# Two-level Strassen mixture of experts on one Trainium2 core: another order of the postponed sums on VectorE, the shares loaded in halves, one more empty place in a list

## The chip, the cores and the metric

The kernel runs on one core of one Trainium2 chip. The metric is the time of one execution on the device in microseconds; of the kernel before there are three runs, and their median counts. One more execution was recorded by the profiler. The engines are named as the profile names them: PE (TensorE, the matrix multiplier), PEld (the loads of its weights, which run beside it), DVE (VectorE), ACT (ScalarE), POOL (GpSimd) and SP (SyncE, which issues most transfers). Each engine works through its own instructions in the order in which they were issued, and waits on semaphores for the others.

## What is computed

Three stages in a row, in float32 throughout:

```python
x = attention(q, k_pooled, v_pooled)            # 4 batches x 576 tokens = 2304 tokens, 512 wide
P = exp(x @ w_gate - max)                       # 2304 x 8 experts
for _ in range(8):                              # Sinkhorn: rows, then columns
    P /= P.sum(1); P /= P.sum(0); P *= 2304 / 8
y = sum(P[:, e] * (relu(x @ w1[e]) @ w2[e]) for e in range(8))     # w1: 512 x 1024, w2: 1024 x 512
out = softplus(y @ w_in) @ w_out                # 512 x 2048, 2048 x 512
```

Nearly all of the time goes into the matrix products of the last two lines. Each float32 product is made of three products of rounded parts: high by high, high by low, low by high, where "low" is the remainder that is left when the high part is taken away.

## The kernel before

**Phases and units.** The 2304 tokens are three parts of 768. The six phases are the experts on part 0, on part 1 and on part 2, and then the softplus layer on parts 1, 2 and 0. In an expert phase there are 32 units, four for each expert, and a unit is 256 columns of the hidden layer. `first` makes a unit's hidden activations, `second` multiplies them by the second matrix and adds into the result.

**Strassen.** A unit's first product is cut into 2 x 2 blocks, and seven block products take the place of eight, at the price of sums of blocks on the other engines. In the phases of parts 1 and 2 (`TWICE`) this is done for the second product too, over two units together, an even one and the odd one behind it: seven products that are called forms 0 to 6 here.

**One pair, in PE's order.** `first_twice` of the even unit makes A11, A22, S2, S1, A12 and S3 (lines 852 to 875). Then `second_twice` of the odd unit of the pair before makes that pair's form 2; `go_on` brings the even unit's seventh product, S4; forms 3 to 6 follow. Then the odd unit comes in the same way, with forms 0 and 1 of its own pair around its S4. Each of the block products is six matrix multiplications of 384 columns, each form twelve.

**The sums of a unit on DVE.** The products lie in PSUM in two tiles of two banks each, d1 (pa and pd) and d2 (pc and pb). ACT copies A11 to `a`. DVE then makes `u1 = pb + a` (row `u<-p,za` in the profile), after S2 and S1, and PE may add S3 onto pb only when u1 has been read. After S3 DVE makes `a = pb + a` (`za<-p,za`), `pb = pc + a` and `pd = pd + a` (both `p<-p,za`, pb's first). PE may add S4 onto pc only when `pb = pc + a` has read pc. After S4 comes `pc = pc + u1` (`p<-p,u`).

**Forms out of sums.** `even_posts` and `odd_posts` multiply the positive part of d1 and d2 by the tokens' shares (`shared`, `p<-p,pb` or `a<-p,pb`; `pb` is here the tile that holds one expert's 768 shares on every partition) and build the seven left factors. The last four steps of the odd unit are put off: the list `later` (line 954) holds s2 (form 5: a cast on ACT, a remainder on POOL), s4 (form 6: `d1 = d1 - s3` on DVE, row `p<-p,s`, then a cast on ACT), s1 (form 4: `a21 = d2 + a21` on DVE, row `a<-p,a`, then a cast on ACT, a remainder on POOL), and form 6's remainder on DVE (`hlo<-p,hhi`, which needs the cast of s4). `first_twice` of the next even unit issues them: the first two ahead of u1, the other two right behind it (lines 860 to 869).

**Shares.** `load_shares` brings the next expert's 768 shares in one transfer by SP, at the end of each fourth unit, when `p2` of that unit has read the old ones. `p1` of the next even unit reads the first half of them, `p2` the second.

**Side work.** While the first phase runs, `hook` takes one entry at a time from the list `side` at fixed places between the products; an entry of None is an empty place. The Sinkhorn steps stand in it: `sk_max` (a maximum on DVE), an empty place, `sk_max_t` (a transpose on PE, row `pm<-ident,big`), and so on. When the list is empty the same places serve the conversion of the last weights from float64 (`convert`).

Of the kernel before, what the change touches and what calls it, by code (L numbers as in the profile page):

```python
# [19 lines left out]
def attention_moe_softplus_kernel(  # L20
# [12 lines left out]
    nc = tc.nc  # L33
    B, H, S, D = q.shape
    N, DM = out.shape
    E = w_gate.shape[1]
# [7 lines left out]
    P = 128  # L44
# [12 lines left out]
    UPE = FF // US  # L57
# [4 lines left out]
    LARGE = max(PAIRS)  # L62
# [110 lines left out]
    TWICE = (1, 2)  # L173
    FORMS = 7
    TB = LARGE // 2
# [6 lines left out]
    pb = []  # L182
    sd = {u: dram.tile([P, 4, 2, P], F32, name=f"sd{u}") for u in range(NU1)}
    td = {d: dram.tile([P, 4, UC, HALF], F32, name=f"td{d}") for d in range(NU1 // 2)}
    pd = dram.tile([sum(PAIRS[1:]) // P * E, P], F32, name="pd")
# [8 lines left out]
    def pair_of_units(n):  # L194
        return TWICE.index(sets[n][0]) * NU1 // 2 + sets[n][3] // 2
# [48 lines left out]
        pool_sub(lo, raw_form(q), hi.bitcast(F32))  # L244
        load_form(q + 4)

    def load_shares(i):
        if i < len(TWICE) * E:
            m, e = divmod(i, E)
            n = LARGE // P  # L250
            src = pd.rearrange("(t e) p -> e t p", e=E)[e, m * n:(m + 1) * n]
            nc.sync.dma_start(
                pb[0].rearrange("p (t n) -> p t n", n=P), src.partition_broadcast(P)
            )

    def load_w(which, n):
# [564 lines left out]
    def product_of(n):  # L821

        whi, wlo = w1_t.pop(n)

        def product(ps, a, b, onto=False):
            hi, lo = xs[b]
            for c in range(2):
                three(
                    ps, (whi[:, a, c, :], wlo[:, a, c, :]), (hi[:, c, :], lo[:, c, :]),
                    c == 0 and not onto, c == 1, onto,  # L830
                )

        return product

    two_t = {}
    later = []

    def run_later():
        while later:
            later.pop(0)()  # L840

    def two_banks(kind, name):
        return banks[kind].tile([P, 2, 512], F32, tag=f"two{kind}", name=name)[:, :, :TB]
# [4 lines left out]
    def first_twice(n, between):  # L848

        product = product_of(n)  # L850
        a, u1 = (zpool.tile([P, TB], F32, tag="z", name=x) for x in ("za", "u1"))
        kind = "RL"[sets[n][3] // 2 % 2]
        d1 = two_banks(kind, "p")
        pa, pd_ = d1[:, 0], d1[:, 1]
        product(pa, A11, "b11")
        between(0)
        product(pd_, A22, "t4")
        nc.scalar.copy(a, pa)
        between(1)
        for _ in range(2):  # L860
            if later:
                later.pop(0)()
        d2 = two_banks(kind, "p")
        pc, pb = d2[:, 0], d2[:, 1]
        product(pb, S2, "t2")
        between(2)
        product(pc, S1, "t1")
        vadd(u1, pb, a)
        run_later()
        between(3)  # L870
        product(pa, A12, "b21", True)
        between(4)
        product(pb, S3, "t3", True)
        vadd(a, pb, a)
        vadd(pb, pc, a)
        vadd(pd_, pd_, a)
        between(5)
        two_t[n] = d1, d2

        def s4():  # L880
            product(pc, S4, "b22", True)
            vadd(pc, pc, u1)

        return s4

    def shared(o, src, j):

        share = pb[0][:, j * TB:(j + 1) * TB].unsqueeze(1).to_broadcast([P, 2, TB])
        nc.vector.scalar_tensor_tensor(o, src, 0.0, share, op0=ALU.max, op1=ALU.mult)  # L889

    def form_hi(q, src):
        nc.scalar.copy(h_slot(q)[0], src)  # L892

    def form_lo(q, src, eng):
        hi, lo = h_slot(q)
        eng.tensor_tensor(lo, src, hi.bitcast(F32), op=ALU.subtract)
# [23 lines left out]
    def odd_posts(n):  # L920

        f, _, _, u = sets[n]
        q = pair_of_units(n) * FORMS
        d1, d2 = two_t.pop(n)

        def p1():
            shared(d1, d1, 0)
            form_hi(q + 2, d1)

        def p2():  # L930
            shared(d2, d2, 1)
            form_hi(q + 3, d2)
            if u % UPE == UPE - 1:
                load_shares(TWICE.index(f) * E + u // UPE + 1)

        def p3():
            form_lo(q + 2, d1, nc.vector)
            form_lo(q + 3, d2, nc.vector)
            vsub(s3_t(), d2, s3_t())

        def s2():
            form_hi(q + 5, s3_t())
            form_lo(q + 5, s3_t(), nc.gpsimd)

        def s1():
            vadd(a21_t(), d2, a21_t())
            form_hi(q + 4, a21_t())
            form_lo(q + 4, a21_t(), nc.gpsimd)

        def s4():  # L950
            vsub(d1, d1, s3_t())
            form_hi(q + 6, d1)

        later.extend([s2, s4, s1, lambda: form_lo(q + 6, d1, nc.vector)])
        return [p1, p2, p3]

    def m_at(f, k):
# [357 lines left out]
    side = []  # L1315
# [3 lines left out]
    def finish_attention():  # L1319
        actx.close()  # L1320
        gp = ctx.enter_context(tc.tile_pool(name="g23", bufs=1))
        for i in (2, 3):
            g_t[i] = gp.tile([P, GW], F32, name=f"g{i}")
        pools.append(ctx.enter_context(tc.tile_pool(name="tmp", bufs=2)))
        side.extend([to_tiles] + [None] * 6 + [to_prob, None, sk_max, None, sk_max_t, None, None, sk_max_b, None])
        for _ in range(ITERS):
            side.extend([sk_rows, None, None, None, sk_cols])
        side.append(shares_out)
        shares_to_raw(range(RAW - 1))
        sp_ = ctx.enter_context(tc.tile_pool(name="shares", bufs=1))  # L1330
        pb.append(sp_.tile([P, 2 * TB], F32, name="pb"))
        open_extra(("f64", [P, 2 * UC * HALF], U32), ("xl", [P, 2 * TB], F32))
        f64_t.append(pools[0].tile([P, 2 * UC * HALF], U32, tag="f64", name="f64", bufs=1))
        f64_t.append(extra["f64"])
# [228 lines left out]
    for step, (what, n) in enumerate(todo):  # L1563

        quiet[0] = NU1 - 2 <= n <= NU1 + 1
        f, kind, pair, u = sets[n]
        if what == "first":
# [10 lines left out]
            if twice(n):  # L1578
# [10 lines left out]
                def between(k):  # L1589

                    for _ in range((0, 1, 0, 1, 1, 3)[k]):
                        if to_split:
                            to_split.pop(0)()
                    if u % 2 == 0:
                        if k == 2:
                            settled()
                        if joins and k == 1:
                            joins.pop(0)()
                        return
                    if joins and k == 2:  # L1600
                        joins.pop(0)()
                    if k == 0:
                        sharing[0] = not side
                        pause[0] = 0
                    if not sharing[0]:
                        hook()
                    elif (k == 0 and (u < NU1 - 1 or twice(n + 1))) or not between_chunks[0]:
                        convert()
# [38 lines left out]
        else:  # L1647
# [46 lines left out]
                pending.pop(0)()  # L1694
            ahead(f, kind, u)
            if f == 0 and u == NU1 - 6:
                load_shares(0)
            if f == 0 and u == NU1 - 6:
                f64_t.pop()
            if twice(n + 1):  # L1700
# [37 lines left out]
```

## Time and profile before

| what | value |
|---|---|
| median of 3 runs | 1955.19 us (1953.75 to 1955.24) |
| the profiled execution, its own time | 1954.04 us |
| its span, first to last instruction | 1952.3 us |
| PE busy | 1928.6 us, 99% of the span |
| DVE busy | 1471.4 us, 75% |
| POOL busy | 1475.1 us, 76% |
| ACT busy | 973.6 us, 50% |
| granted TensorE clock, mean | 0.999 |

The profiled execution lies 1.15 us below the median of the three runs. A busy PE is no proof of a PE at its peak, since matrix multiplications overlap and their ends are modelled: whether PE lost time is read from the distance between the starts of two that follow each other. In a timeline a row holds the start in us, the duration, the engine and line, the operation, what it writes and reads, and in brackets how long the engine was idle before it and who ended that.

### The profile page before, as it was taken

The numbers are of one execution on the slowest core, as the hardware profiler recorded it, in microseconds if no ns is written. First come the engines' busy times: TensorE is split into PE (matmuls) and PEld (weight loads), VectorE is DVE, ScalarE is ACT, GpSimd is POOL, SyncE is SP. The second block draws the span as 40 slices with busy tenths as digits, with TensorE's granted clock in tenths as the row PEclk, the third lists the DMA queues.
The fourth block names the chain that finished last, engine by engine and source line by source line (L and its number), as shares of the span: only waits on it lengthen the run. The fifth ranks groups of instructions, "written<-read, shape, count | busy, mean of one in ns | idle before, by whom it ended". The sixth has DMA issues, their size and how long they took to land.

```text
span 1952.3 us, 30469 instructions
## 1 busy us (share of the span) xinstructions
PE 1928.6 (99%) x10954; PEld 1794.4 (92%) x10954; DVE 1471.4 (75%) x2339; ACT 973.6 (50%) x1773; POOL 1475.1 (76%) x1142
## 2 busy tenths in 40 slices
PE   9899999999999999999999999999999999999999
PEld 7687888989989999999999999999999999999997
DVE  7775576887667888878988889888789776556455
ACT  6545435433334545545445655455554565565542
POOL 6776667787877788778787798887787879675563
PEclk9999999999999999999999999999999999999999
DMA  7343434555547655554555655555545523523311
GB/s 205 116 150 125 145 125 136 178 178 173 183 151 260 208 165 166 168 181 150 163 176 160 219 168 167 161 174 165 181 153 163 192 93 122 191 89 119 133 65 65
DMA packets 213347, 306.56 MB, mean 157 GB/s; under 512 B 33308, under 2 KB 147532, under 8 KB 212940
## 3 DMA queue, kind: packets, MB, share of 16 engines
q1 hardware_dynamic: 203116, 290.85, 46.4%
q10 hardware_dynamic: 10080, 13.77, 1.9%
q8 instruction: 86, 1.41, 0.3%
q14 instruction: 65, 0.53, 0.1%
HBM read 239.30 MB, written 65.27 MB: 156 GB/s over the span
## 4 chain that ended last, share of the span: by engine, by line
PE 90%; DVE 3%; POOL 2%; ACT 2%; DMA 1%; issue 1%; SPq 0%; ACTq 0%; DVEq 0%; POOLq 0%
PE py L797 45%; PE p L797 42%; POOL w1lo L289 1%; PE px L522 1%; PE s L477 1%; DMA vt<-in_v_dram 1%; PE pa L512 1%; DMA pb<-pd 0%; DVE p L1045 0%; POOL w2lo L289 0%; ACT w1hi L320 0%; DMA w2raw<-td 0%; PE pq L464 0%; ACT xhi L693 0%; DVE za L1045 0%
## 5 line engine op out<-in xcount | busy, mean ns | idle before, releaser
L797 PE MATMUL p<-xhi,w1hi 128*128 128x384 f32 x1680 | 572.7, 341 | 5.1 <-DVE p L1045 1.3
L797 PE MATMUL p<-xlo,w1hi 128*128 128x384 f32 x1680 | 563.0, 335 | 0.1
L797 PE MATMUL p<-xhi,w1lo 128*128 128x384 f32 x1680 | 562.9, 335 | 0.0
L289 POOL TENSOR_TENSOR w2lo<-w2raw,w2hi 128x512 fp32r<-128x512 f32 (+1 forms) x235 | 364.0, 1566 | 113.0 <-ACT w2hi L243 100.0
L289 POOL TENSOR_TENSOR w1lo<-w1raw,w1hi 128x512 fp32r<-128x512 f32 x240 | 239.6, 1021 | 227.0 <-ACT w1hi L320 226.9
L797 PEld LDWEIGHTS p<-xhi,w1hi 128*128 128x128 f32 x1680 | 315.6, 188 | 30.1 <-DVE u L845 14.0
L797 PEld LDWEIGHTS p<-xlo,w1hi 128*128 128x128 f32 x1680 | 315.7, 188 | 5.0 <-DVE xlo L1399 0.4
L797 PEld LDWEIGHTS p<-xhi,w1lo 128*128 128x128 f32 x1680 | 315.5, 188 | 0.0
L289 POOL TENSOR_TENSOR w1lo<-sums,w1hi 128x1024 fp32r<-128x1024 f32 x120 | 289.1, 2409 | 1.9 <-ACT w1hi L320 1.9
L797 PE MATMUL py<-w2hi,hhi 128*128 128x512 f32 x672 | 266.4, 396 | 3.3 <-DVE kbd L420 1.3
L797 PE MATMUL py<-w2hi,hlo 128*128 128x512 f32 x672 | 264.0, 393 | 0.0
L797 PE MATMUL py<-w2lo,hhi 128*128 128x512 f32 x672 | 263.6, 392 | 0.0
L797 PE MATMUL py<-hhi,w2hi 128*128 128x384 f32 x716 | 239.4, 334 | 1.1 <-ACT whi L243 1.1
L797 PE MATMUL py<-hlo,w2hi 128*128 128x384 f32 x716 | 239.2, 334 | 0.0
L797 PE MATMUL py<-hhi,w2lo 128*128 128x384 f32 x716 | 239.2, 334 | 0.0
L845 DVE TENSOR_TENSOR g<-py,g 128x768 f32<-128x768 f32 x210 | 199.6, 950 | 50.1 <-PE py L797 50.1
L892 ACT CAST hhi<-p 128x768 fp32r<-128x768 f32 x128 | 102.8, 803 | 211.0 <-DVE p L889 205.7
L797 PEld LDWEIGHTS py<-w2hi,hhi 128*128 128x128 f32 x672 | 126.4, 188 | 32.9 <-issue 3.6
L797 PEld LDWEIGHTS py<-w2hi,hlo 128*128 128x128 f32 x672 | 126.4, 188 | 27.0
L797 PEld LDWEIGHTS py<-w2lo,hhi 128*128 128x128 f32 x672 | 126.5, 188 | 22.5
L797 PEld LDWEIGHTS py<-hhi,w2hi 128*128 128x128 f32 x716 | 134.4, 188 | 1.5 <-ACT whi L243 1.3
L797 PEld LDWEIGHTS py<-hhi,w2lo 128*128 128x128 f32 x716 | 134.4, 188 | 0.0
(163 smaller groups left out, 3540.3 us busy)
## 6 DMA issues: line engine op xcount, KB each, us to landing
w1raw<-in_moe_w_dram SPq DMA_DIRECT2D x96, 512.0 KB
w2raw<-td SPq DMA_DIRECT2D x128, 256.0 KB
sums<-sd SPq DMA_DIRECT2D x62, 512.0 KB
w2raw<-in_moe_w_dram SPq DMA_DIRECT2D x96, 256.0 KB
w2raw<-in_moe_w_dram SPq DMA_DIRECT2D x32, 512.0 KB
sd<-sums SPq DMA_DIRECT2D x32, 512.0 KB
td<-w2raw SPq DMA_DIRECT2D x64, 256.0 KB
xlo<-xlod SPq DMA_DIRECT2D x35, 384.0 KB
```

Of the source, the lines that this page charges most:

```text
L289: nc.gpsimd.tensor_tensor(o, a, b, op=ALU.subtract)
L477: nc.tensor.matmul(ps[:QP, j * 2 * SP:(j + 1) * 2 * SP], qT[:, j * QP:(j + 1) * QP], kb)
L512: nc.tensor.transpose(pa[:SP, j * QP:(j + 1) * QP], ex[:, 2 * j + h, :], ident[:QP, :QP])
L522: nc.tensor.matmul(px[h * D:(h + 1) * D, :W], vp[:, h, :], aT[:, h, :])
L797: nc.tensor.matmul(ps, lhs[a], rhs[b], start=first and i == 0, stop=last and i == 2, skip_group_check=goes_on,)
L845: vadd = lambda o, x, y: nc.vector.tensor_tensor(o, x, y, op=ALU.add)
L892: nc.scalar.copy(h_slot(q)[0], src)
```

## The change

Four things are edited. In `first_twice` one step of `later` is issued ahead of u1 and not two; two steps follow u1 and not all that are left; what then remains is issued behind `a = pb + a`. In `odd_posts` the list `later` is s2, s1, s4 and form 6's remainder, and not s2, s4, s1 and the remainder. `load_shares` brings 384 shares at a time: the first half is issued when `p1` of the fourth unit has read its half, the second when `p2` has. In `side` one more empty place stands between `sk_max` and `sk_max_t`.

```diff
@@ load_shares
-    def load_shares(i):
+    def load_shares(i, j):
         if i < len(TWICE) * E:
             m, e = divmod(i, E)
-            n = LARGE // P
-            src = pd.rearrange("(t e) p -> e t p", e=E)[e, m * n:(m + 1) * n]
+            n = TB // P
+            t = m * 2 * n + j * n
+            src = pd.rearrange("(t e) p -> e t p", e=E)[e, t:t + n]
             nc.sync.dma_start(
-                pb[0].rearrange("p (t n) -> p t n", n=P), src.partition_broadcast(P)
+                pb[0][:, j * TB:(j + 1) * TB].rearrange("p (t n) -> p t n", n=P), src.partition_broadcast(P)
             )
@@ first_twice
         between(1)
-        for _ in range(2):
-            if later:
-                later.pop(0)()
+        if later:
+            later.pop(0)()
         d2 = two_banks(kind, "p")
         pc, pb = d2[:, 0], d2[:, 1]
         product(pb, S2, "t2")
         between(2)
         product(pc, S1, "t1")
         vadd(u1, pb, a)
-        run_later()
+        for _ in range(2):
+            if later:
+                later.pop(0)()
         between(3)
         product(pa, A12, "b21", True)
         between(4)
         product(pb, S3, "t3", True)
         vadd(a, pb, a)
+        run_later()
         vadd(pb, pc, a)
         vadd(pd_, pd_, a)
@@ odd_posts
+        def next_shares(j):
+            if u % UPE == UPE - 1:
+                load_shares(TWICE.index(f) * E + u // UPE + 1, j)
+
         def p1():
             shared(d1, d1, 0)
             form_hi(q + 2, d1)
+            next_shares(0)
 
         def p2():
             shared(d2, d2, 1)
             form_hi(q + 3, d2)
-            if u % UPE == UPE - 1:
-                load_shares(TWICE.index(f) * E + u // UPE + 1)
+            next_shares(1)
...
-        later.extend([s2, s4, s1, lambda: form_lo(q + 6, d1, nc.vector)])
+        later.extend([s2, s1, s4, lambda: form_lo(q + 6, d1, nc.vector)])
@@ finish_attention
-        side.extend([to_tiles] + [None] * 6 + [to_prob, None, sk_max, None, sk_max_t, None, None, sk_max_b, None])
+        side.extend([to_tiles] + [None] * 6 + [to_prob, None, sk_max, None, None, sk_max_t, None, None, sk_max_b, None])
@@ the loop over the units, first phase
-                load_shares(0)
+                load_shares(0, 0)
+                load_shares(0, 1)
```

What this does to DVE in the even unit of each pair is shown for the second pair of the second phase. The rows run from the odd unit's two remainders to the even unit's p1; `s` is the tile of the second sums' difference, `a_` with a number is a21, `za` is `a`. Before:

```order
L896 TENSOR_TENSOR hlo_883<-p,hhi_882 128x768 x2
L846 TENSOR_TENSOR s_6713<-p,s_6713 128x768
L846 TENSOR_TENSOR p<-p,s_6713 128x2x384
L845 TENSOR_TENSOR u_7253<-p,za 128x384
L845 TENSOR_TENSOR a_6712<-p,a_6712 128x768
L896 TENSOR_TENSOR hlo_1146<-p,hhi_1145 128x768
L845 TENSOR_TENSOR za<-p,za 128x384
L845 TENSOR_TENSOR p<-p,za 128x384 x2
L889 SCALAR_TENSOR_TENSOR p<-p,pb 128x2x384
```

And the same stretch of DVE now:

```order
L899 TENSOR_TENSOR hlo_883<-p,hhi_882 128x768 x2
L847 TENSOR_TENSOR s_6714<-p,s_6714 128x768
L846 TENSOR_TENSOR u_7255<-p,za 128x384
L846 TENSOR_TENSOR a_6713<-p,a_6713 128x768
L847 TENSOR_TENSOR p<-p,s_6714 128x2x384
L846 TENSOR_TENSOR za<-p,za 128x384
L899 TENSOR_TENSOR hlo_1146<-p,hhi_1145 128x768
L846 TENSOR_TENSOR p<-p,za 128x384 x2
L892 SCALAR_TENSOR_TENSOR p<-p,pb 128x2x384
```

The subtraction of s4 (`p<-p,s`) has moved from ahead of u1 to behind s1, and form 6's remainder (`hlo<-p,hhi`) from ahead of `za` to between `za` and the two additions that follow it. PE's order in a pair is the same as before.

On ACT, from the copy of A11 to the casts of the next weights, before:

```order
L858 COPY za<-p 128x384
L892 CAST hhi_1145<-s_6713 128x768
L892 CAST hhi_1145<-p 128x768
L892 CAST hhi<-a_6712 128x768
L320 CAST w1hi<-w1raw 128x512
```

And now:

```order
L859 COPY za<-p 128x384
L895 CAST hhi_1145<-s_6714 128x768
L895 CAST hhi<-a_6713 128x768
L895 CAST hhi_1145<-p 128x768
L321 CAST w1hi<-w1raw 128x512
```

The cast that form 6's remainder needs (`hhi<-p`) now stands behind that of s1 (`hhi<-a`), as its subtraction does on DVE.

## Rows read from the trace of the kernel before

**Rows 1.** The page, part 1: busy time, share of the span, instructions.

```profile
PE 1928.6 (99%) x10954; PEld 1794.4 (92%) x10954; DVE 1471.4 (75%) x2339; ACT 973.6 (50%) x1773; POOL 1475.1 (76%) x1142
```

**Rows 2.** Waits of the weight loads: total us, times, longest us.

```profile
PEld p L797 <- DVE u L845: 14.0, 48, 0.6
```

**Rows 3.** Timeline of DVE in an even unit, 673 to 681 us.

```profile
673.35 0.95 DVE L846 TENSOR_TENSOR s<-p,s 128x768 f32<-128x768 f32 x1
674.33 0.97 DVE L846 TENSOR_TENSOR p<-p,s 128x768 f32<-128x768 f32 x1
675.21 0.55 DVE L845 TENSOR_TENSOR u<-p,za 128x384 f32<-128x384 f32 x1
675.67 0.95 DVE L845 TENSOR_TENSOR a<-p,a 128x768 f32<-128x768 f32 x1
676.54 0.95 DVE L896 TENSOR_TENSOR hlo<-p,hhi 128x768 fp32r<-128x768 f32 x1
677.40 0.55 DVE L845 TENSOR_TENSOR za<-p,za 128x384 f32<-128x384 f32 x1
677.98 1.03 DVE L845 TENSOR_TENSOR p<-p,za 128x384 f32<-128x384 f32 x2
679.05 0.97 DVE L889 SCALAR_TENSOR_TENSOR p<-p,pb 128x768 f32<-128x768 f32 x1
680.29 0.57 DVE L845 TENSOR_TENSOR p<-p,u 128x384 f32<-128x384 f32 x1 [0.27 <-PE p L797]
```

**Rows 4.** Timeline of PE in the same unit, from S1's last multiplication to S4's.

```profile
674.42 0.33 PE L797 MATMUL p<-xhi,w1lo 128*128 128x384 f32 x1
...
675.46 0.34 PE L797 MATMUL p<-xhi,w1lo 128*128 128x384 f32 x1
675.81 0.44 PE L797 MATMUL p<-xhi,w1hi 128*128 128x384 f32 x1
676.09 0.34 PE L797 MATMUL p<-xlo,w1hi 128*128 128x384 f32 x1
...
676.79 0.33 PE L797 MATMUL p<-xhi,w1lo 128*128 128x384 f32 x1
...
679.05 0.33 PE L797 MATMUL p<-xhi,w1hi 128*128 128x384 f32 x1
...
679.91 0.33 PE L797 MATMUL p<-xhi,w1lo 128*128 128x384 f32 x1
```

**Rows 5.** Timeline of the weight loads at S3's start.

```profile
675.29 0.19 PEld L797 LDWEIGHTS p<-xhi,w1lo 128*128 128x128 f32 x1
675.81 0.19 PEld L797 LDWEIGHTS p<-xhi,w1hi 128*128 128x128 f32 x1 [0.33 <-DVE u L845]
```

**Rows 6.** Timeline of ACT in the same unit: the cast of s4.

```profile
675.33 0.80 ACT L892 CAST hhi<-p 128x768 fp32r<-128x768 f32 x1 [0.17 <-DVE p L846]
```

**Rows 7.** Timeline of PE one pair earlier: S1's last multiplication.

```profile
645.29 0.33 PE L797 MATMUL p<-xhi,w1lo 128*128 128x384 f32 x1
```

**Rows 8.** Timeline of DVE in that earlier pair: u1 waiting for PE.

```profile
645.73 0.56 DVE L845 TENSOR_TENSOR u<-p,za 128x384 f32<-128x384 f32 x1 [1.05 <-PE p L797]
```

**Rows 9.** Timeline of DVE at the start of the third phase.

```profile
1095.52 0.97 DVE L889 SCALAR_TENSOR_TENSOR p<-p,pb 128x768 f32<-128x768 f32 x1 [1.95 <-DMA pb<-pd]
```

**Rows 10.** Timeline of PE there: form 3's last multiplication, form 4's first.

```profile
1096.56 0.34 PE L797 MATMUL py<-hhi,w2lo 128*128 128x384 f32 x1
1097.95 0.41 PE L797 MATMUL py<-hhi,w2hi 128*128 128x384 f32 x1 [1.06 <-ACT whi L243]
```

**Rows 11.** Timeline of SP there: sums and tokens for the next unit, then the shares.

```profile
1085.63 0.32 SPq L282 DMA_DIRECT2D sums<-sd  x1
1086.04 0.38 SPq L695 DMA_DIRECT2D xlo<-xlod  x1
1086.52 0.38 SPq L252 DMA_DIRECT2D pb<-pd  x1
```

**Rows 12.** Timeline of PE in the first phase: the transpose of the maxima.

```profile
241.73 0.27 PE L1184 MATMUL pm<-ident,big 128*1 128x128 f32 x1 [0.88 <-DVE big L1180]
```

## The prediction

> **What bounds the kernel now.** The page's busy times come first: PE is busy for 99% of the span [rows 1], so a gain or a loss must be a gap between PE's starts. The list of who waited for whom comes second. In the two phases that the change touches, the largest entry is a weight load that waits for DVE's u1: 14.0 us over 48 waits [rows 2]. The timelines come third, and they say what these waits cost.
>
> In an even unit PE's multiplications start 0.17 us apart. At S3 the first starts 0.35 us after its forerunner (675.46 to 675.81), and the second another 0.28 us later (676.09) [rows 4]: (0.35 - 0.17) + (0.28 - 0.17) = 0.29, from unrounded starts 0.28 us lost. The weight load of that multiplication stood idle for 0.33 us until u1 was read [rows 5]; u1 ran from 675.21 to 675.76 and the load began at 675.81 [rows 3, 5], a handover of 0.05. The extra 0.11 on the second start is what a restart costs once the load had to wait. The same picture stands in 28 of the 32 pairs, 29 to 30 us apart: 28 x 0.28 = 7.8 us. The other 20 of the 48 waits lie in odd units, where `later` is empty; the change leaves them alone.
>
> Why is u1 late? DVE is never idle from 673.35 to 679.05; s4's subtraction ends just ahead of u1 [rows 3]. So the edit sees a real stall. The question is what is late next.
>
> **The change part by part: the order of the sums.** I put DVE's new order on the clock of that pair, with PE not stalled at S3.
>
> u1 can't simply move up by the 0.87 us of the subtraction. One pair earlier DVE had nothing ahead of u1 and sat idle 1.05 us until 645.73 [rows 8]; PE started S1's last multiplication at 645.29 [rows 7]. So u1 waits for S1, which lies in the same two-bank tile, and starts 0.44 after its last start. (The shortest such handover here is 679.91 to 680.29, 0.38 [rows 3, 4].) In our pair S1's last start is 674.42 [rows 4], so u1 starts at 674.86 and is done at 675.41. S3's load comes without a stall a sixth of a us ahead of 675.63, at about 675.48, so S3 runs on time. That part is a gain of 0.28.
>
> Now the rest of DVE's row, each step from start to start as in rows 3. s1 comes 0.46 after u1: 675.32. s4's subtraction comes 0.87 after s1: 676.19, and it takes 0.97: 677.16. ACT's cast starts 0.03 after its end (674.33 + 0.97 = 675.30, cast at 675.33) and takes 0.80 [rows 3, 6]: 677.19 to 677.99. ACT is free by then: s1's sum is done at 676.27, and its cast is of the same size. In the meantime DVE has made `za` from about 677.07, the subtraction's usual 0.88 behind its start; S3's data have been there since 0.38 behind its last start, now 676.79 - 0.28 = 676.51: 676.89. The next instruction is form 6's remainder, which needs that cast: with 0.03 for the handover it starts at 678.02, and DVE is idle for half a us ahead of it.
>
> Behind the remainder are queued `pb = pc + a`, `pd = pd + a` and p1. PE waits for the first: S4 may start only when it has read pc. It starts 0.86 after the remainder (676.54 to 677.40 is that distance [rows 3]), at 678.88, and takes 0.55: 679.43; with 0.05 the weight load goes at 679.48. Before, S4 started at 679.05, thirteen steps of 0.174 behind S3's last multiplication at 676.79 [rows 4], so without a gap; with 0.28 less ahead of it, it would now start at 678.77. It is late by 0.71, plus the restart's 0.11: 0.82 us. Taking 0.38 for u1's handover gives 0.76; a remainder that gets its cast 0.05 later gives 0.87. **So a stall of 0.28 at S3 is exchanged for one of 0.82 at S4: +0.54 for each of 28 pairs, +15.1 us** (0.48 to 0.59: 13.4 to 16.5).
>
> Downstream: p1 starts 0.87 later than before and PE is 0.54 later, so p1 is 0.33 later against PE. In the one place where p1 was late enough to stop form 4 it was 1.95 us late and cost 1.3 us [rows 9, 10], so some 0.6 of lateness was free. I cost this at nothing. DVE catches up during forms 3 to 6. s1's own start is 0.35 earlier, and its sum is done at 676.27, ahead of form 2, which takes the bank.
>
> The two pairs at the beginning of the two phases had no stall at S3 (rows 8 is one of them) and get the one at S4: 2 x 0.82 = +1.6. The pair across the border of the phases had next to none at S3 either: +0.8. The last odd unit's sums fall into the softplus phase, where `first` calls them at one place; form 6's remainder waits for a later cast there too: between 0 and +0.4, I take +0.2.
>
> **The shares.** One wait of DVE for this transfer reached PE. At the border of the phases the transfer went out at 1086.52 [rows 11], p1 began at 1095.52 after 1.95 idle [rows 9], and form 4 began 1.39 us after its forerunner instead of 0.17, 1.3 with its restart [rows 10]. Elsewhere the first half can leave as soon as the odd unit's p1 is done. Here it stands in SP's queue behind the transfer of sums that goes at 1085.63, so it leaves at about 1086.0, only 0.5 earlier; but it is half as long, and the 384 KB of tokens that went at 1086.04 now come behind it [rows 11]. By the 0.5 alone p1 would be late by 1.95 - 0.5 = 1.4, less the 0.87 by which the new order puts it back anyway: 0.6, about the free lateness. So the stall goes, or all but a little of it: I take -1.2, with bounds -1.3 and 0. The other half is needed by p2 alone, some 2 us later than p1. The added issue, under 0.4 us of SP, has no other wait between the halves except that one transfer of tokens.
>
> **The empty place.** The transpose of the maxima waits 0.88 us for DVE [rows 12]. One place later PE has a tile of `second` and a block product ahead of it, over 2 us of work, so the wait goes: -1.0 with its restart. All later Sinkhorn steps and the conversion move by a place too; the same kind of step could wait elsewhere. Bounds -1.1 and +1.0.
>
> **Sum:** 15.1 + 1.6 + 0.8 + 0.2 - 1.2 - 1.0 = +15.5 us. On the profiled execution's own 1954.0 this gives 1969.5. That execution was 1.15 below the median of the runs, so against the runs it is 1970.7, if the difference is more than chance; I say **1970**.
>
> [...] Independent additions start 0.86 to 0.87 us apart though each lasts 0.95 [rows 3], so the next starts before the last has ended. [...]
>
> **The rivals.** *1. S4 does not wait.* If the remainder held nothing up, the change would do only what its S3 side shows: 1954.0 - 7.8 - 1.2 - 1.0 = 1944, on the other side. It decides at one point: `pb = pc + a` must be over some 0.8 us earlier than I put it, at 678.6. Without the wait for the cast the remainder would start at 677.53 and the addition end at 678.94, still too late. So it takes a u1 that starts half a us ahead of S1's end, against rows 7 and 8. Chance 0.05.
>
> *2. The two stalls nearly cancel.* If u1 only waited for S2, DVE's row would stay packed, the subtraction would end at 676.5 and the cast at 677.4; `pb = pc + a` would end at 678.8, some 0.2 lost at S4 against 0.28 at S3. Then 28 x -0.06 + 3 x 0.2 - 2.2 = -3.3 gives some 1951, and 1955 at a loss of 0.35. Rows 7 and 8 speak against it. Chance 0.05.
>
> *3. DVE runs end to end.* Three steps of the row (u1 to s1, s1 to s4, remainder to addition) each grow by 0.09: S4 loses 0.26 more in 31 pairs, +8, some 1978. The 0.86 of rows 3 speak against it. Chance 0.03.
>
> *4. Something further down is late as well.* The 0.33 by which p1 falls back against PE may be more than the slack of form 2's accumulation on DVE, which PE needs before form 4, or of the weights' casts behind p1's cast on ACT. By my row the accumulation starts at 681.3 and is over 0.25 ahead of form 4's load. If that goes, 0.2 to 0.4 more in 31 pairs: 1976 to 1982. Chance 0.08.
>
> **How the numbers follow.** The forecast has 0.79, and its own range comes from the ends above: 13.4 to 16.5 for the pairs, 0 to 0.4 for the last, -1.3 to 0 for the shares, -1.1 to +1.0 for the empty place, and the median's spread of 1.5 us: 1966 to 1975. To hold 8 in 10 the range takes in the lower half of rivals 3 and 4: **1964 to 1977**. A measurement of this kernel can tell about 0.2%, 3.9 us, from no change. Faster: rival 1 and a quarter of rival 2, 0.06. Same: the rest of rival 2, 0.04. Slower: 0.90.
>
> **What would show it.** In the profile after, u1 no longer follows the subtraction but waits for PE, some 0.6 us idle; S3 starts 0.17 after A12's last multiplication; DVE is idle about 0.5 us ahead of form 6's remainder until ACT's cast; and S4's weight load waits for `p<-p,za` some 0.9 us in 31 pairs, over 20 us in the list of waits. p1 no longer waits for the shares and the transpose no longer for the maximum. I am wrong if S4 follows form 2 without a gap, or if PE's gaps in a pair sum to less than before.

## The result, and the profile after

The changed kernel takes 1970.1 us (median of 4 runs, 1969.2 to 1974.5), the kernel before 1955.2 us in the same session. The ratio is 1.0082, with a 95% interval from 1.0064 to 1.0099: 14.9 us slower, against a forecast of 1970 us, 15.5 above the profiled execution. The profiled execution of the changed kernel took 1969.17 us. Executions of one kernel often fall into two groups 4 to 5 us apart (in experiment 7 1941.6 to 1942.5 and 1946.4 us; in the profiled ones of experiments 5, 8 and 12 PE has 46 multiplications between 4.5 and 10 us, in that of the changed kernel 82), so differences of a few us are read from PE's gaps below.

First the page's row of busy times (as in [rows 1]) and two rows of the list of waits: what waited, for what, total us, times, longest us.

```profile
PE 1928.8 (98%) x10954; PEld 1794.9 (91%) x10954; DVE 1470.0 (75%) x2339; ACT 973.1 (49%) x1773; POOL 1475.0 (75%) x1142
...
PEld p L798 <- DVE p L846: 27.8, 32, 1.0
...
PEld p L798 <- DVE u L846: 5.0, 22, 0.3
```

No engine has noticeably more work than before; PE is busy for 1928.8 us as against 1928.6. What grew is time in which it waits. The wait for u1 [rows 2] fell from 14.0 us in 48 waits to 5.0 in 22, and a new entry of 27.8 us in 32 waits stands in front: weight loads that wait for an addition, `p<-p,za`, 1.0 us at worst.

The pair of [rows 3 to 6] in the changed kernel, on DVE, with idle time ahead of a row in brackets:

```profile
674.34 0.56 DVE L846 TENSOR_TENSOR u<-p,za 128x384 f32<-128x384 f32 x1 [0.56 <-PE p L798]
674.81 0.95 DVE L846 TENSOR_TENSOR a<-p,a 128x768 f32<-128x768 f32 x1
675.68 0.96 DVE L847 TENSOR_TENSOR p<-p,s 128x768 f32<-128x768 f32 x1
676.54 0.55 DVE L846 TENSOR_TENSOR za<-p,za 128x384 f32<-128x384 f32 x1
677.50 0.96 DVE L899 TENSOR_TENSOR hlo<-p,hhi 128x768 fp32r<-128x768 f32 x1 [0.41 <-ACT hhi L895]
678.37 1.02 DVE L846 TENSOR_TENSOR p<-p,za 128x384 f32<-128x384 f32 x2
679.43 0.97 DVE L892 SCALAR_TENSOR_TENSOR p<-p,pb 128x768 f32<-128x768 f32 x1
```

ACT's cast of s4, S4's first weight load, and PE's form 2 and S4 in that pair:

```profile
676.67 0.80 ACT L895 CAST hhi<-p 128x768 fp32r<-128x768 f32 x1
```

```profile
678.98 0.19 PEld L798 LDWEIGHTS p<-xhi,w1hi 128*128 128x128 f32 x1 [0.90 <-DVE p L846]
```

```profile
678.06 0.34 PE L798 MATMUL py<-hhi,w2lo 128*128 128x384 f32 x1
678.99 0.44 PE L798 MATMUL p<-xhi,w1hi 128*128 128x384 f32 x1 [0.58 <-DVE p L846]
679.27 0.34 PE L798 MATMUL p<-xlo,w1hi 128*128 128x384 f32 x1
```

u1 waits for PE and S3 is no longer late. The cast ends at 677.47, form 6's remainder begins at 677.50, and behind it `pb = pc + a` is done 0.55 after 678.37. PE's last multiplication of form 2 starts at 678.06 and S4's first 0.93 later instead of 0.17; its second start is 0.28 later, 0.11 more than usual. That is 0.86 us; it is 0.83 to 0.92 in the 31 pairs, up to 0.86 in 28 of them.

A table for the two expert phases that the change touches makes the kernels comparable. A gap is the distance between two starts on PE beyond the usual one for that shape (0.174 us for 384 columns), summed where it is over 0.04, restarts with the place that they belong to. It is worked out from all of PE's rows between 575 us and the end of the third phase. The last column is PE's wait for the tokens' low parts (`xlo`) near the border of the two phases.

| kernel | all gaps, us | u1 (S3) | S4 | first loads of forms | tokens |
|---|---|---|---|---|---|
| before | 15.5 | 11.8 in 48 | - | 1.5 | 0.2 |
| changed | 31.6 | 4.0 in 22 | 26.1 in 31 | - | - |
| 1, remainder behind | 12.7 | 4.5 in 22 | 0.3 | 6.1 in 53 | 0.3 |
| 2, s4 ahead of s1 | 26.9 | 4.4 in 22 | - | 19.4 in 31 | 1.4 |
| 3, order alone | 32.6 | 4.0 in 22 | 26.5 in 31 | 0.6 | - |
| 4, one conversion later | 22.8 | - | 15.1 in 24 | 5.7 in 48 | 0.6 |
| 5, results added first | 8.8 | 4.8 in 22 | 0.2 | 0.6 | 1.5 |
| 6, no use of the cast | 31.6 | 4.0 in 22 | 26.1 in 31 | - | - |
| 7, conversion earlier | 4.7 | 0.6 in 2 | 0.7 in 2 | 0.6 | 1.3 |
| 8, shares alone | 15.0 | 12.3 in 49 | - | - | 0.7 |
| 9, remainder from sums | 54.3 | 4.1 in 22 | 48.6 in 31 | - | - |
| 10, old order, swaps | 11.1 | 8.2 in 29 | - | - | 1.3 |
| 11, empty place alone | 15.9 | 12.7 in 49 | - | 1.4 | - |
| 12, another bank | 21.1 | 4.0 in 22 | 14.5 in 32 | - | 1.0 |

Every kernel also has a gap of 1.4 at the end of the third phase and one or two small ones ahead of 641 us, which no column holds. What stands under S4 for experiments 1, 5 and 7 are gaps of 0.24 to 0.39 in the softplus phase behind it; 4 and 12 hold one of these too.

From before to after the gaps grew by 31.6 - 15.5 = 16.1 us in these phases, the span by 1967.4 - 1952.3 = 15.1.

### The profile page after: what moved, and what is told of

The parts are those of the page before. It is cut to its first block, busy times and chain, and to the rows that moved or that the text cites. A ratio compares the mean times of both kernels' runs of the same rounds, so it can differ in the third digit from the quotient of the medians.

```text
span 1967.4 us, 30489 instructions
## 1 busy us (share of the span) xinstructions
PE 1928.8 (98%) x10954; PEld 1794.9 (91%) x10954; DVE 1470.0 (75%) x2339; ACT 973.1 (49%) x1773; POOL 1475.0 (75%) x1142
## 4 chain that ended last, share of the span: by engine, by line
PE 85%; DVE 8%; ACT 3%; issue 3%; POOL 1%; DMA 0%; ACTq 0%; DVEq 0%; POOLq 0%
PE py L798 42%; PE p L798 40%; DVE p L847 2%; ACT hhi L895 1%; DVE hlo L899 1%; DVE p L846 1%; DVE u L846 1%; PE s L478 1%; PE px L523 1%; PE pa L513 1%; PE pk L433 0%; POOL w1lo L290 0%; ACT w1hi L321 0%; PE pq L465 0%; POOL w2raw L290 0%
## 5 line engine op out<-in xcount | busy, mean ns | idle before, releaser
L798 PEld LDWEIGHTS p<-xhi,w1hi 128*128 128x128 f32 x1680 | 315.9, 188 | 48.5 <-DVE p L846 27.8
L899 POOL TENSOR_TENSOR hlo<-s,hhi 128x768 fp32r<-128x768 f32 x64 | 118.7, 1855 | 37.7 <-ACT hhi L895 36.3
```

The lines of the kernel that those rows point to most:

```text
L798: nc.tensor.matmul(ps, lhs[a], rhs[b], start=first and i == 0, stop=last and i == 2, skip_group_check=goes_on,)
```

## Experiments on what holds S4

**1. The remainder behind the additions.** One line of the changed kernel moves:

```diff
         vadd(a, pb, a)
-        run_later()
         vadd(pb, pc, a)
         vadd(pd_, pd_, a)
+        run_later()
```

> The changed kernel with one line moved: form 6's remainder is issued behind the unit's three additions and not between them. Theory (what is queued behind the waiting remainder holds PE): the addition pb = pc + a starts 0.58 us behind za, as it did before the change, so near 677.1 on the clock of the changed kernel's pair, and S4's weight load, due at 678.24, no longer waits. The remainder starts near 678.1, its cast long done, and is done near 679.1, just ahead of form 3's first load, which needs its bank (due near 679.28). 31 stalls of 0.83 to 0.86 us go: 1970 - 31 x 0.84 = 1944 us, about 11 below the kernel before, and the weight loads no longer stand in the list of waits with 27.8 us for DVE's additions. Rival A (PE waits there for something else as well, say p1 or form 3's load behind the later remainder): a stall of 0.3 to 0.5 comes back at form 3 or 4, 1952 to 1960. Rival B (S4 was late for another reason, such as S3's own end): about 1970, unchanged.

Measured: 1953.2 us, ratio to before 0.9995 (0.9986 to 1.0003). The 31 stalls at S4 are gone, so the queue behind the remainder was the cause and rival B falls. But the time fell by 17 us and not by 26: rival A. DVE and the weight loads in the same pair (S4 starts at 678.32 here, without a gap):

```profile
677.21 1.03 DVE L846 TENSOR_TENSOR p<-p,za 128x384 f32<-128x384 f32 x2
678.14 0.95 DVE L899 TENSOR_TENSOR hlo<-p,hhi 128x768 fp32r<-128x768 f32 x1
679.01 0.96 DVE L892 SCALAR_TENSOR_TENSOR p<-p,pb 128x768 f32<-128x768 f32 x1
679.87 0.56 DVE L846 TENSOR_TENSOR p<-p,u 128x384 f32<-128x384 f32 x1
680.34 0.95 DVE L846 TENSOR_TENSOR g<-py,g 128x768 f32<-128x768 f32 x1
```

```profile
681.09 0.19 PEld L798 LDWEIGHTS py<-hhi,w2lo 128*128 128x128 f32 x1
681.40 0.19 PEld L798 LDWEIGHTS py<-hhi,whi 128*128 128x128 f32 x1
```

p1 now starts 0.69 after S4's first multiplication (679.01 against 678.32). It was 0.00 in the kernel before (679.05 in both [rows 3, 4]) and 0.44 in the changed one. With it slips `g<-py,g`, the addition that takes form 2's result out of the bank that form 4 needs: it ends at 681.29, and form 4's load goes at 681.40, 0.31 after its forerunner instead of 0.17. Such gaps make 6.1 us.

**5. The results added first.** The kernel of experiment 1 with two swaps in `second_twice`: form 2's result goes to its total ahead of `go_on`'s addition, form 4's ahead of form 0's remainder.

```diff
                 if posts:
                     posts.pop(0)()
-                go_on()
-            onto()
-            if posts:
+                onto()
+                go_on()
+            else:
+                onto()
+            if posts and k < 4:
                 posts.pop(0)()
             elif pending:
                 pending.pop(0)()
-            if k == 3 and posts:
+            if k == 4 and posts:
                 posts.pop(0)()
```

> The first experiment's kernel (remainder behind the additions) with two more swaps on VectorE in the forms of an odd unit: form 2's result is added to its total ahead of the addition p = p + u, and form 4's result ahead of form 0's remainder. In the first experiment the stall at S4 is gone, but PE loses 6.3 us in 88 small gaps at the first loads of forms 4 and 6, which take the banks that DVE must empty by these two additions (at 680.34 and 684.66, done at 681.29 and 685.61; the loads went at 681.40 and 685.72 instead of 681.26 and 685.5). Theory (a backlog on DVE is what took back 6 of the 26 us): both additions come 0.47 and 0.87 earlier, the 88 gaps go, 1953.2 - 6 = 1947 us, some 7 below the kernel before. Rival A (the gaps come from the late weight casts on ACT, which the trace names at some of them): unchanged, 1953. Rival B (p2's or form 0's postponed remainder becomes late and stops PE elsewhere): 1950 to 1957.

Measured: 1947.5 us, ratio 0.9964 (0.9951 to 0.9977), and 0.6 us of gaps at the forms instead of 6.1. The backlog on DVE is what took the gain back. The trace names ACT's casts at some of those gaps, but their order is the same here and the gaps are gone, so rival A falls.

**2. s4 ahead of s1.**

```diff
-        later.extend([s2, s1, s4, lambda: form_lo(q + 6, d1, nc.vector)])
+        later.extend([s2, s4, s1, lambda: form_lo(q + 6, d1, nc.vector)])
```

> The changed kernel with s4's subtraction and cast put back ahead of s1's; the remainder stays between the unit's additions. It separates the remainder's wait for ACT's cast from its own 0.86 us in DVE's queue. Theory (both add up): the cast is ready 0.87 us earlier, the remainder starts without idle time at about 677.0 instead of 677.50, the addition ends near 678.4 instead of 678.94, and S4's load, due at 678.24, is late by 0.2 plus the restart's 0.11. A stall of 0.32 in 31 pairs instead of 0.84: 1970 - 31 x 0.52 = 1954 us. Rival A (the cast alone makes the stall): S4 does not wait, 1944. Rival B (DVE runs end to end, each step 0.09 longer): the stall is 0.6, 1962. Rival C (the late cast costs nothing): 1970.

Measured: 1965.4 us, ratio 1.0053 (1.0037 to 1.0069): none of the four. The list of waits says why:

```profile
PEld py L798 <- DVE a L846: 20.9, 31, 0.7
```

Form 2 takes the bank that s1's sum must read first, and that sum now comes 0.87 later. The stall moved from S4 to form 2, 0.63 a pair, and PE was then late enough for S4. The run says nothing on the cast; it shows that s1 has a due time too, which the order of the change respects.

**6, 9 and 12. How much of it is the wait for the cast.** In all three the instruction of form 6's remainder stays at its place and is given other operands:

```diff
-        later.extend([s2, s1, s4, lambda: form_lo(q + 6, d1, nc.vector)])
+        later.extend([s2, s1, s4, lambda: vsub(h_slot(q + 6)[1], d1, a21_t())])       # 6
+        later.extend([s2, s1, s4, lambda: vsub(h_slot(q + 6)[1], s3_t(), a21_t())])   # 9
+        later.extend([s2, s1, s4, lambda: form_lo(q + 6, d1, nc.vector) if now[0] is None else vsub(h_slot(q + 6)[1], now[0], a21_t())])  # 12
...
         vadd(a, pb, a)
+        now[0] = d2                         # 12: this unit's own d2
         run_later()
+        now[0] = None
```

> The changed kernel, with its order, but form 6's remainder subtracts s1's sum (done long before) and not its own rounded value, so it no longer waits for ACT's cast. This leaves the rounding remainder of form 6 out of the result; the instruction has the same size and place. It separates the wait for the cast from the remainder's own time in the queue. Theory (the two add up): the remainder starts 0.46 behind za, at 677.00 instead of 677.50, the addition pb ends at 678.44 instead of 678.93, and S4's load, due at 678.24, is late by 0.25 plus the restart's 0.11: 0.36 instead of 0.84 in 31 pairs, 1970 - 15 = 1955 us. Rival A (the whole stall is the late cast): S4 does not wait, 1944. Rival B (the cast is not what the remainder waits for, it is the order of DVE itself): 1970.

Measured: 1970.3 us, ratio 1.0070 (1.0057 to 1.0083), as the changed kernel. The wait had not gone:

```profile
677.08 0.96 DVE L847 TENSOR_TENSOR hlo<-p,a 128x768 fp32r<-128x768 f32 x1 [0.41 <-ACT hhi L895]
```

DVE still begins at s4's bank 0.03 behind the end of ACT's cast of it (676.25 + 0.80 = 677.05), although both only read; over the run it waits 13.7 us in 32 waits for the cast, as in the changed kernel. The wait belongs to the bank and not only to the data: in experiments 9 and 12 the same instruction writes to the same place, reads other tiles, and starts 0.46 behind the start of `za` without idle time.

> The experiment before on the cast left the wait in place: an instruction on DVE that reads the bank of s4's sum still began only when ACT's cast of the same bank was done (0.41 idle, as in the changed kernel), though it used nothing that the cast writes. Here the remainder's instruction reads two sums in the on-chip buffer, s3's and s1's, and touches neither the bank nor the rounded value, so form 6's rounding remainder is left out of the result; place and size are as in the changed kernel. Theory (the wait for the cast and the remainder's own time add up): no idle time ahead of it, it starts 0.46 behind za, pb's addition ends near 678.44 and S4's load is late by 0.25 plus the restart: 0.36 instead of 0.84 in 31 pairs, 1955 us. Rival A (the cast is the whole of the stall): 1944. Rival B (the idle time is tied to something else in DVE's row): 1970.

Measured: 1993.8 us, ratio 1.0200 (1.0185 to 1.0215). The remainder began at once, 0.46 behind `za`, but took 2.36 us here and 2.14 on the mean of 32. DVE's row and two of POOL's beside it:

```profile
678.47 2.36 DVE L847 TENSOR_TENSOR hlo<-s,a 128x768 fp32r<-128x768 f32 x1
```

```profile
678.18 1.84 POOL L899 TENSOR_TENSOR hlo<-a,hhi 128x768 fp32r<-128x768 f32 x1
679.98 2.68 POOL L290 TENSOR_TENSOR w1lo<-w1raw,w1hi 128x512 fp32r<-128x512 f32 x2
```

S4 lost 48.6 / 31 = 1.57 a pair. By the sum of wait and own time it should lose 0.36, plus what the longer instruction adds, 2.14 - 0.96 = 1.18: 1.54. The time was far off the forecast, since I had taken 0.96 for it; the sum itself, by which every us of the remainder reaches S4, held.

> The two experiments before on the cast did not hold its size: the first still waited for ACT on the bank of s4's sum, the second read two operands from the on-chip buffer and took 2.36 us instead of 0.96. Here form 6's remainder reads the bank of S1 and S3 of its own unit and s1's sum: one operand from a bank and one from the buffer, as in the changed kernel, same size and place, and neither s4's bank nor the rounded value. Form 6's rounding remainder is left out of the result. Theory (wait and own time add up): no idle time ahead of it, it starts 0.46 behind za, at 677.00 on the changed kernel's clock. The addition pb = pc + a now overwrites what it reads, so it starts 0.04 behind its end and not 0.09 ahead: 678.00, done 678.55. S4's load, due at 678.24, goes at 678.60: 0.36 and the restart's 0.11, 0.47 instead of 0.84 in 31 pairs, 1970 - 31 x 0.37 = 1958 us. Rival A (the cast is the whole of the stall): S4 does not wait, 1944. Rival B (the cast is none of it): 1970 or more.

Measured: 1962.6 us, ratio 1.0029 (1.0016 to 1.0042). In its trace the remainder takes 0.95 again, nothing is idle ahead of it, and the addition follows 0.03 behind its end:

```profile
681.14 0.55 DVE L847 TENSOR_TENSOR za<-p,za 128x384 f32<-128x384 f32 x1
681.60 0.95 DVE L848 TENSOR_TENSOR hlo<-p,a 128x768 fp32r<-128x768 f32 x1
682.58 1.03 DVE L847 TENSOR_TENSOR p<-p,za 128x384 f32<-128x384 f32 x2
```

S4 loses (14.5 - 0.25) / 31 = 0.46 a pair, where 0.47 was forecast; the gaps fell from 31.6 to 21.1, 10.5 us, and by 11.5 without the 1.0 us that PE waits for tokens here, which is the 31 x 0.37 of the forecast. The median is 4.6 us above the forecast of 1958; the wait for tokens is 1.0 of it, and the rest does not lie in these phases. So of the 0.84 a pair about 0.5 is the wait for the cast (0.38 shown, and 0.11 more, worked out, since the addition starts 0.98 behind the remainder here and 0.87 in the changed kernel), and the rest is the remainder's own time ahead of the addition.

## Experiments on the other parts

**3, 8 and 11. The three parts alone**, each put into the kernel before: the order of the sums, the shares in halves, the empty place (their pieces of the diff above).

> The kernel before with the new order of the sums alone; shares in one piece, the old list of places. Theory: all of the loss comes from here: 28 x 0.54 + 2 x 0.82 + 0.8 + 0.2 = +17.7 us, 1973 us, 2.2 to 3 us over the changed kernel, and the wait for the shares at the border of the phases (1.3 us) and the one of the transpose of the maxima (1.1 us) are there again. Rival A (the shares in halves made part of the loss, by more packets or a later p1): below 1970. Rival B (the two other edits gave nothing): 1970.

Measured: 1972.4 us, ratio 1.0091 (1.0077 to 1.0104). The whole loss is the order's. The two other parts should make the 2.3 us between 1972.4 and 1970.1, too little for the runs alone; the gaps differ by 1.0 us in the two phases (32.6 and 31.6) and by 1.3 from 200 to 560 us. At the border of the phases only 0.44 of the 1.30 us is left even with the shares in one piece: p1 comes later in the new order and waits 0.76 us for them, not 1.95 [rows 9].

```profile
1104.35 0.97 DVE L891 SCALAR_TENSOR_TENSOR p<-p,pb 128x768 f32<-128x768 f32 x1 [0.76 <-DMA pb<-pd]
```

> The kernel before with the shares loaded in halves alone. Theory: the one wait at the border of the phases (form 4's load 1.2 late and a restart, 1.3 us) goes or nearly goes, all else stays: 1955 - 1.2 = 1954 us, which only the trace can show. Rival A (the first half still lands late, since the order of the sums, which puts p1 back by 0.87, is what hides it in the changed kernel): some 0.3 to 0.9 us of the stall remains. Rival B (the halves have smaller packets and hold up the tokens behind them): a new wait for xlo at the start of the phase, 0.2 to 1.3 us.

Measured: 1954.3 us, ratio 0.9987 (0.9978 to 0.9996). Form 4's wait is gone whole, so rival A falls, but the trace has rival B's wait: the tokens that now stand between the two halves in SP's queue go 0.89 behind the transfer of sums (1090.28 and 1091.17) and not 0.41 [rows 11], and PE waits 0.43 for them.

```profile
1099.03 0.45 PE L798 MATMUL p<-xlo,w1hi 128*128 128x384 f32 x1 [0.43 <-DMA xlo<-xlod]
```

With its restart that costs 0.70. In the changed kernel this wait does not exist; PE is held at S4 there by 0.83, which may hide it, but that was not tried apart. It is there in every kernel with the halves whose stall at S4 is smaller or gone (last column of the table), for example in experiment 5:

```profile
1096.40 0.44 PE L798 MATMUL p<-xlo,w1hi 128*128 128x384 f32 x1 [1.03 <-DMA xlo<-xlod]
```

In experiments 2, 5, 7 and 10 it makes 1.3 to 1.5 us, as much as the wait of 1.30 that stood there before. No run has one of these kernels with the shares in one piece.

> The kernel before with one more empty place ahead of the transpose of the maxima alone. Theory: PE's wait of 1.13 us there goes, and the steps behind it, all a place later, cost 0.3 more in one transpose of the shares (0.55 instead of 0.22 in the changed kernel): 1955 - 0.8 us, too little for the clock of the runs, so the gaps in the trace decide. Rival A (other steps wait instead, about as long): the gaps sum to as much as before. Rival B (a step of the loop meets another tile and waits longer): up to 1 us slower.

Measured: 1954.9 us, ratio 0.9999 (0.9990 to 1.0008). PE's wait of 1.13 us ahead of `pm` is gone, and 0.33 came at a transpose of the shares at 300 us (0.31 in the kernel before, 0.64 here); two gaps near 330 us, 0.85 together, became one of 0.34. PE's gaps from 200 to 560 us fell from 6.35 to 5.26: a gain of 1.1 that the runs cannot tell.

**4 and 7. The 22 waits that are left for u1.** They lie in odd units, where DVE converts weights. Experiment 4 moves a piece of the conversion from ahead of u1 to behind it, experiment 7 moves the first piece ahead of the last form's addition; 4 starts from experiment 1, 7 from experiment 5.

```diff
         product(pb, S2, "t2")
-        between(2)
         product(pc, S1, "t1")
         vadd(u1, pb, a)
+        between(2)                          # 4
```

```diff
             else:
+                if k == FORMS - 1 and early[0]:
+                    early[0]()              # 7: the piece that between(0) of the odd unit ran
                 onto()
...
```

> The first of these kernels (remainder behind the additions) and one line more: in the units that split their conversions, the conversion at the third place is issued behind u1 and not ahead of it. In the profile of the changed kernel S3's first load still waits for u1 in 20 odd units, 0.06 us plus 0.11 for the restart. Theory (the conversion ahead of u1 makes it late): these 20 waits go, 20 x 0.17 = 3.4 us, 1941 us if the first kernel takes 1944. Rival A (u1 is late in odd units because of its handover from PE alone): no change against the first kernel. Rival B (the conversion, now later, keeps another engine waiting: its consumers or the following additions): 1945 to 1950.

Measured: 1963.1 us, ratio 1.0048 (1.0034 to 1.0061). u1 is in time, and 24 stalls at S4 of odd units took the place of its 22, 15.1 us instead of 4.5: the piece is two instructions of 0.69 on DVE, now queued ahead of `pb = pc + a`. Rival B, far dearer than I had put it, and by the mechanism of the change itself.

> The kernel with the two swaps and one more: the first piece of the conversion that an odd unit runs on DVE is issued ahead of the last form's addition instead of behind it, where DVE is idle for 1.28 us (686.86 to 688.14 in the first experiment). Theory (u1 is late in 22 odd units since DVE runs packed from that addition to u1): u1 starts when PE's S1 lets it, and 22 waits of 0.2 us, 4.4 in all, go: 4 us less than the kernel without it, 1943 if that one takes 1947. Rival A (u1 then still waits, for ACT's part of the conversion): the same as without. Rival B (the conversion delays the last form's addition, and PE waits for its bank): 3 to 6 us more than without.

Measured: 1942.5 us, ratio 0.9935 (0.9924 to 0.9947). It beats both kernels, the one before by 12.7 us by the ratio. The two instructions fill idle time ahead of the last form's addition, and u1 waits for PE:

```profile
686.47 0.69 DVE L1272 TENSOR_SCALAR da<-f 128x512 uint32<-128x512 uint32 x1
687.20 0.70 DVE L1275 SCALAR_TENSOR_TENSOR da<-f,da 128x512 uint32<-128x512 uint32 x1
687.80 0.95 DVE L847 TENSOR_TENSOR g<-py,g 128x768 f32<-128x768 f32 x1
...
691.79 0.56 DVE L847 TENSOR_TENSOR u<-p,za 128x384 f32<-128x384 f32 x1 [0.90 <-PE p L798]
```

**10. The old order in that kernel.** Experiment 7 with the postponed sums as in the kernel before: s2 and s4 ahead of u1, s1 and the remainder behind it.

```diff
-        if later:
-            later.pop(0)()
+        for _ in range(2):
+            if later:
+                later.pop(0)()
...
-        for _ in range(2):
-            if later:
-                later.pop(0)()
+        run_later()
...
         vadd(pb, pc, a)
         vadd(pd_, pd_, a)
-        run_later()
...
-        later.extend([s2, s1, s4, lambda: form_lo(q + 6, d1, nc.vector)])
+        later.extend([s2, s4, s1, lambda: form_lo(q + 6, d1, nc.vector)])
```

> The seventh experiment's kernel (1942.5 us) with the postponed sums in the order of the kernel before: s2 and s4 ahead of u1, then s1 and form 6's remainder, then the additions. It asks what the new order of the sums is worth once nothing queued behind it stops PE. Theory (the order alone removes the stall of S3, as in the prediction's first step): S3 is late again by 0.28 in 28 pairs, 7.8 us, and nothing else changes: 1950 us. Rival A (with the other swaps u1 is in time in either order, the gain came from them alone): 1942.5. Rival B (more is lost, in S4 or form 3): over 1953.

Measured: 1949.1 us, ratio 0.9974 (0.9961 to 0.9987), 6.6 us above experiment 7, and 7.6 by the two ratios. The waits for u1 are back:

```profile
PEld p L798 <- DVE u L847: 9.6, 29, 0.3
```

So the new order, with one sum ahead of u1 and not two, is worth 7.6 us of gaps (8.2 against 0.6) once nothing behind it stops PE.

## Why the prediction was right, point by point

| step | forecast, us | in PE's gaps |
|---|---|---|
| S3 in even units | -7.8 | 11.8 to 4.0: -7.8 |
| S4 in 31 pairs | 31 x 0.82 = +25.4 | +26.1 |
| last odd unit, in the softplus phase | +0.2 | +0.27 |
| shares, border of the phases | -1.2 | -1.30 |
| empty place | -1.0 | -1.1 (experiment 11) |

- **u1 waits for S1.** 0.56 idle ahead of u1, as forecast (some 0.6). This decided against rival 2.
- **The late cast and the queue.** Forecast: the remainder 2.70 behind s1, `pb` 3.56, S4's load late by 0.71 and a restart of 0.11. Measured: 2.69 and 3.56, and 0.72 to 0.75 with 0.11 in 28 of the 31 pairs. The profile's idle time, which counts from the end of `za`, is 0.41; the prediction's own row gives 678.02 - 677.62 = 0.40 for it, and its half a us counts from where the remainder could have started without the wait. Experiments 1, 9 and 12 show both halves of the mechanism, the queue and the wait.
- **Nothing further down.** p1 fell back by 0.44 against S4's first multiplication, that is 0.33 against PE behind the restart of 0.11, as forecast, and cost nothing. Experiment 1 shows how near the edge that is: at 0.69, without a restart, form 4's and form 6's loads wait. Rival 4 was the right place with the right engine, at most 0.36 us away. I had not seen this when I expected 1944 us of experiment 1.
- **Rival 3.** Independent sums still start 0.87 apart though each lasts 0.95 (674.81 and 675.68), so DVE did not run end to end and rival 3 falls. The addition `pb = pc + a` starts 0.03 behind the end of `za`, whose result it needs [rows 3], and 0.03 behind the end of the remainder in experiment 12, where it overwrites what that reads; in the changed kernel, where it does neither, it starts 0.87 behind the remainder's start, and so 0.09 ahead of its end.
- **Shares.** The size was right in the changed kernel, in part by luck. That the order itself takes away much of the wait was in the forecast, and the order alone removes two thirds of it (experiment 3). But the prediction let the tokens wait behind the first half and took that at nothing. In the kernel before it is not nothing: the halves give 0.6 there and not 1.2 (experiment 8).

## What to carry to other kernels

Ahead of moving a step up in an engine's queue, look at what the step that now waits has behind it: an instruction that waits for a cast costs its idle time and its own time, less the slack that was there, to everyone who waits for what is queued after it (here 0.84 us a pair at S4, about 0.5 of it for the cast). Issue first what another engine waits for, then what waits for others; the reordering that lost 15 us is worth 7 once the remainder, two additions and a piece of conversion stand in the order of their due times (experiments 7 and 10). Such a move uses up slack further down (p1 fell back from 0.00 to 0.44 and, in experiment 1, to 0.69 behind S4's first multiplication), so the expectation must carry the new lateness to the next place where banks are handed over.

## What the runs showed of the hardware

A subtraction of 128 x 768 on DVE, form 6's remainder, took 0.95 us with one operand in PSUM and one in the on-chip buffer (experiment 12), but 2.14 us on the mean of 32 with both in the buffer (experiment 9). It is not the two operands alone: the last of the 32 took 0.95 too. It began when POOL's own instruction had 0.02 us left. Three others lasted as long as what was left of POOL's instruction at their start, and 0.81 to 0.82 more: 2.36 where 1.55 was left, in the rows of experiment 9 above, 1.73 where 0.92 was left, 1.01 where 0.19 was. Here is the second of them, with POOL's two instructions beside it, and the last one:

```profile
740.03 1.73 DVE L847 TENSOR_TENSOR hlo<-s,a 128x768 fp32r<-128x768 f32 x1
...
739.09 1.86 POOL L899 TENSOR_TENSOR hlo<-s,hhi 128x768 fp32r<-128x768 f32 x1
740.91 2.55 POOL L899 TENSOR_TENSOR hlo<-a,hhi 128x768 fp32r<-128x768 f32 x1
...
1604.51 0.95 DVE L847 TENSOR_TENSOR hlo<-s,a 128x768 fp32r<-128x768 f32 x1
```

POOL's next work was longer in turn: 2.55 here and 2.68 in the rows of experiment 9, where the same steps took 1.84 and 1.98 in the changed kernel's pair of [rows 3 to 6]. Why both were longer, no run shows.
